# Centring the first tile ahead of its transposes, scaling it behind V, and loading V's weights in 256 KB chunks

## The chip, the cores and the metric

The kernel runs on one core of one Trainium2 chip. The metric is the device time of one execution in microseconds; the time before is the median of three runs. A core has a matrix engine (TensorE, PE in the profile; its weight loads are PEld), a vector engine (VectorE, DVE), a scalar engine (ScalarE, ACT), a general engine (GpSimd, POOL) and SyncE (SP), which here only issues DMAs. Each engine works through its own queue in order, and engines wait for each other through semaphores. Matrix products go to PSUM; from there VectorE or ScalarE copies them to SBUF.

## The reference

Two kinds of layer are applied twice in turn to x, which has 2048 tokens of 1024 features in bf16. Both have a layer norm without gain ahead of them and a residual addition behind them. Shapes are shortened here.

```
def _layernorm(x, eps=1e-5):
    return (x - mean(x)) / sqrt(var(x) + eps)

def _A_ref(x, wqkv, wo):          # 32 heads of 32, window of 8 keys, 2 tokens apart
    q, k, v = split_heads(x @ wqkv)
    logits = einsum("bhsd,bhswd->bhsw", q, gather(k)) * scale     # masked below token 0
    o = einsum("bhsw,bhswd->bhsd", softmax(logits), gather(v))
    return merge_heads(o) @ wo

def _B_ref(x, W_gate, W_up, W_down):
    gate = x @ W_gate
    h = gate * (gate > 0) * (x @ W_up)
    return h @ W_down

x = x + _A_ref(_layernorm(x), A_wqkv, A_wo)
x = x + _B_ref(_layernorm(x), B_W_gate, B_W_up, B_W_down)
x = x + _A_ref(_layernorm(x), A_wqkv, A_wo)
x = x + _B_ref(_layernorm(x), B_W_gate, B_W_up, B_W_down)
```

Only the first layer norm, of the first 512 tokens, and the V product behind it are touched by the change.

## The kernel before

The tokens are cut into tiles of 128 (`x_tiles`) and into blocks of four tiles; four blocks and two layer pairs make eight passes. In each pass come the norm, Q, K and V, the windowed attention on VectorE, the output projection, and the gated feed-forward. Weights come as slabs through a ring of five buffers (`load_slab`). The order of the work is written out by hand: every step is an event with a due time in us, the events are sorted, and each engine's instructions are chained in that order (`dv` for VectorE, `sp_dma` for SyncE's DMA queue, `pe_group` for TensorE, `on` in the first norm for ScalarE, GpSimd and VectorE).

The change lies in the start of block 0, where nothing can yet be overlapped. `load_x(0, ...)` fetches the first tiles of x; tile 0 comes in two halves, one on SyncE's queue and one on ScalarE's. The V weights come as two slabs `("v0", 0)` and `("v0", 1)`, each with four of the eight 128-row chunks of the contraction (`kc`), each in two DMAs of 512 KB.

`ln_first` normalises the four tiles of block 0. `scratch` issues matmuls on a constant while TensorE has nothing else. For tiles 0, 1 and 3, `bn` and `aggr` get mean and variance on VectorE; for tile 2, ScalarE gets the sum of squares and the mean (`act_square`, `act_mean`). `power` turns a variance into the reciprocal standard deviation (`rstd`) with two small GpSimd instructions. `apply` subtracts the mean and multiplies by `rstd` on VectorE, `turn` transposes the tile by eight TensorE transposes into PSUM, and `copy` brings the result to SBUF (`xnT`). Behind its matrices stand the second tile's transposes (`second`) and those of tiles 2 and 3 (`later`).

`v_first` then orders V's products so that they can begin with tile 0 alone. `prod(kc, c, t0, t1)` multiplies one contraction chunk by one of eight groups of 128 V columns (`c`) for tiles t0 to t1. `head` does contraction chunks 0 to 3 for tile 0 and slips in tile 1's transposes; `first_half(t)` does the same chunks for tiles 1, 2 and 3; `second_half(i, t0)` does chunks 4 to 7 for two tiles at once (256 columns) and ScalarE copies the finished accumulators out. The sums of tiles 0 and 1 share four PSUM buffers (`pairs`), those of tiles 2 and 3 four others; six buffers of that kind exist. After V come Q and K of block 0 (`qk_steps`), which read all four tiles of `xnT`, starting with Q's first column group.

In the chain of events the order of V's steps is: `head`, `first_half(1)`, `second_half(0..3, 0)` with tile 2's transposes ahead of i = 2, `first_half(2)` with tile 3's transposes in its middle, `first_half(3)`, `second_half(0..3, 2)`.

Of the kernel before, what the change touches and what calls it, by code (L numbers as in the profile page):

```python
# [8 lines left out]
F32 = mybir.dt.float32  # L9
ALU = mybir.AluOpType  # L10
ACT = mybir.ActivationFunctionType
AX = mybir.AxisListType

P = 128
D = 1024
# [5 lines left out]
KC = D // P  # L21
# [4 lines left out]
SLAB = 512  # L26
# [10 lines left out]
def kernel(  # L37
# [117 lines left out]
    eps_col = const.tile([P, 1], F32, name="eps_col")  # L155
    nc.gpsimd.memset(eps_col[:], EPS)
    NTOK = HALO + S
    v_d = dram.tile([H * DH, NTOK], BF16, name="v_d")
    o_d = dram.tile([NT, H, DH, P], BF16, name="o_d")
    q_d = dram.tile([KC, P, S], BF16, name="q_d")  # L160
# [10 lines left out]
    def load_x(b, tiles=range(TPB)):  # L171
        for t in (b * TPB + i for i in tiles):
            if t == 0:
                sp_dma(x_tiles[t][:, 0:SLAB], x_dram[t * P:(t + 1) * P, 0:SLAB])
                nc.scalar.dma_start(x_tiles[t][:, SLAB:D], x_dram[t * P:(t + 1) * P, SLAB:D])
            else:
                sp_dma(x_tiles[t][:], x_dram[t * P:(t + 1) * P, :])

# [41 lines left out]
    def load_slab(key, src):  # L220
        shp = list(src.shape)
        t = wring.tile([P, 8 * SLAB], BF16, tag="slab", name="w_" + "_".join(str(k) for k in key))
        tv = t[:, 0:shp[1] * shp[2]].rearrange("p (a b) -> p a b", b=shp[2])
        if key[0] == "v0":
            for i in range(2):
                rows = slice(i * (KC // 4), (i + 1) * (KC // 4))
                start = nc.scalar.dma_start if (key[1], i) == (0, 1) else sp_dma
                start(tv[:, rows, :], src[:, rows, :])
        else:
            sp_dma(tv, src)  # L230
        slab[key] = tv
# [69 lines left out]
        return mv, rstd  # L301

    load_slab(("v0", 0), qkv_half(2, 0))
    load_x(0, [2, 3])
    load_slab(("v0", 1), qkv_half(2, 1))
    load_slab(("qk01", "q", 0), qkv_half(0, 0))

# [3 lines left out]
    def scratch(count):  # L311
        sc = psum_l.tile([P, W, P], F32, tag="L", name="scratch")
        for _ in range(count):
            with pe_group():
                mm(sc[:, 0:WH, :], lhsT=ones[:, 0:P], rhs=ones[:], start=True, stop=True)

    def ln_first():
        hold = {"xnT": xnT_pool.tile([P, TPB, KC, P], BF16, tag="xnT", name="xnT_first")}
        xna = big_tile([P, TPB, D], "xn_first", True)
        last = {}  # L320

        def on(eng, f, *args, **kwargs):
            if eng == "v":
                dv(f, *args, **kwargs)
            elif eng in last:
                with tc.issue_after(last[eng]):
                    last[eng] = f(*args, **kwargs).ins
            else:
                last[eng] = f(*args, **kwargs).ins

        def small(name, bufs=4):
            return stat_pool.tile([P, 1], F32, tag="f" + name, name=name, bufs=bufs)

        mean, rstd, bst, sq = {}, {}, {}, {}

        def bn(t, half):
            if half == 0:
                bst[t] = stat_pool.tile([P, 2, 6], F32, tag="bst", name="bst")
            on("v", nc.vector.bn_stats, bst[t][:, half, :], x_tiles[t][:, half * SLAB:(half + 1) * SLAB])

        def aggr(t):
            mv = stat_pool.tile([P, 2], F32, tag="mv", name="mv", bufs=4)
            on("v", nc.vector.bn_aggr, mv[:], bst[t][:].rearrange("p a b -> p (a b)"))
            mean[t] = mv[:, 0:1]
            power(t, mv[:, 1:2], 1.0)

        def power(t, var, sign):
            rstd[t], vpe = small("rstd1"), small("vpe1")
            on("g", nc.gpsimd.tensor_scalar, vpe[:], var, sign, EPS, op0=ALU.mult, op1=ALU.add)
            on("g", nc.gpsimd.tensor_tensor, rstd[t][:], vpe[:], neg_half[:, 0:1], op=ALU.pow)  # L350

        def act_square(t):
            sq[t] = small("sq1")
            on("a", nc.scalar.activation, xna[:, t, :], x_tiles[t][:], ACT.Square, scale=float(D) ** -0.5,
               accum_out=sq[t][:])

        def act_mean(t):
            mn = small("mean1")
            on("a", nc.scalar.activation, xna[:, t, :], x_tiles[t][:], ACT.Identity, scale=1.0 / D, accum_out=mn[:])
            mean[t] = mn[:]  # L360

        def act_power(t):
            nvar = small("nvar1")
            on("v", nc.vector.scalar_tensor_tensor, nvar[:], mean[t], mean[t], sq[t][:], op0=ALU.mult, op1=ALU.subtract)
            power(t, nvar[:], -1.0)

        def apply(t, half=None):
            cols = slice(0, D) if half is None else slice(half * SLAB, (half + 1) * SLAB)
            on("v", nc.vector.tensor_scalar, xna[:, t, cols], x_tiles[t][:, cols], mean[t], rstd[t][:],
               op0=ALU.subtract, op1=ALU.mult)  # L370

        tps = {}

        def turn(t, halves=(0, 1)):
            if t in tps:
                pass
            elif t == 0:
                tps[t] = [psum.tile([P, KC // 2, P], BF16, tag="acc", name=f"tp{h}")[:] for h in range(2)]
            else:
                both = psum_l.tile([P, 2, KC, P], BF16, tag="L", name="tp_pair")  # L380
                tps[t] = [both[:, h, 0:KC // 2, :] for h in range(2)]
                if t == 1:
                    tps[t][1] = psum.tile([P, KC // 2, P], BF16, tag="acc", name="tp_second")[:]
            for c in (h * (KC // 2) + i for h in halves for i in range(KC // 2)):
                with pe_group():
                    tail_pe[0] = nc.tensor.transpose(tps[t][c // (KC // 2)][:, c % (KC // 2), :],  # L386
                                                     xna[:, t, c * P:(c + 1) * P], ident[:]).ins

        def copy(t, eng, h, i0=0, i1=KC // 2):
            f = nc.vector.tensor_copy if eng == "v" else nc.scalar.copy  # L390
            on(eng, f, hold["xnT"][:, t, h * (KC // 2) + i0:h * (KC // 2) + i1, :], tps[t][h][:, i0:i1, :])

        warm = small("warm")
        on("a", nc.scalar.activation, warm[:], ones[:, 0:1], ACT.Identity)
        scratch(13)
        bn(0, 0)
        bn(0, 1)
        aggr(0)
        bn(1, 0)
        apply(0, 0)  # L400
        apply(0, 1)
        turn(0)
        copy(0, "a", 0, 0, KC // 4)
        copy(0, "a", 0, KC // 4, KC // 2)
        act_square(2)
        act_mean(2)
        bn(1, 1)
        aggr(1)
        copy(0, "v", 1)
        apply(1, 0)  # L410
        apply(1, 1)

        def second(h):
            turn(1, (h,))
            copy(1, "v", h)
            if h == 0:
                return
            bn(3, 0)
            act_power(2)
            bn(3, 1)  # L420
            aggr(3)
            apply(2)
            apply(3)

        hold["second"], hold["last"] = second, last
        hold["later"] = {t: (lambda t=t: (turn(t), copy(t, "a", 0), copy(t, "v", 1))) for t in (2, 3)}
        return hold


# [2 lines left out]
    def v_steps(n, ln, key, early=False):  # L432
# [15 lines left out]

        return [f_(c) for c in range(KC)]

    def v_first(ln):
        st = att[0]
        pairs, opened = {}, set()
# [11 lines left out]

        def head():
            st["vT"] = big_tile([P, KC, BLK], "vT_0", True)
            for kc in range(KC // 2):
                for c in range(KC):
                    if (kc, c) == (KC // 2 - 1, KC // 2):  # L470
                        ln["second"](0)
                    prod(kc, c, 0, 1)
            ln["second"](1)

        def first_half(t):
            def f():
                for c in range(KC):
                    if t == 2 and c == KC // 2:
                        ln["later"][3]()
                    for kc in range(KC // 2):  # L480
                        prod(kc, c, t, t + 1)
            return f

        def second_half(i, t0):
            def f():
                if (i, t0) == (2, 0):
                    ln["later"][2]()
                for c in (2 * i, 2 * i + 1):
                    for kc in range(KC // 2, KC):
                        prod(kc, c, t0, t0 + 2)  # L490
                tail_act[0] = nc.scalar.copy(st["vT"][:, 2 * i:2 * i + 2, t0 * P:(t0 + 2) * P],
                                             pairs.pop((t0 // 2, i))[:]).ins
            return f

        tail = [(GRP * (2 + 4 * part + 0.5 * i), second_half(i, 2 * part)) for part in range(2) for i in range(KC // 2)]
# [598 lines left out]
```

## Time and profile before

| What | Value |
|---|---|
| median of three runs | 1618.01 us |
| lowest and highest run | 1617.66 and 1618.36 us |
| span of the profiled execution, first to last instruction | 1616.8 us |
| median less that span | 1.2 us |
| TensorE busy | 1610.6 us (100% of the span) |
| VectorE, ScalarE, GpSimd busy | 70%, 29%, 11% |
| TensorE busy from 0 to 24 us | 21.64 us |
| DMA share from 4 to 20 us, by stretches of 2 us | 1.02 to 1.06 |
| granted TensorE clock | 1.00 |

The profile shows one execution, whose own time is not given beside its span; the runs are taken without it, and 1.2 us lie between the span and their median. A row of the timeline begins with the start in us from the span's start and the duration; then come engine, line, operation, written tile and read tiles, shape, and the number of instructions merged. In brackets stands how long the engine was idle before, and what ended that. Line numbers are those of the code above; many operations share the line of a helper (L106 `dv`, L327 `on`, L132 `mm`). "Landing" of a DMA is counted from the start of its issue.

### The profile page before, as it was taken

The page shows a single profiled execution, that of the slowest core. Times are in us where ns is not written, and L with a number is a line of the kernel's source. Part 1 is how long each engine was busy: PE and PEld are TensorE (multiplying, and loading weights), DVE is VectorE, ACT ScalarE, POOL GpSimd, SP SyncE. Part 2 cuts the span into 40 slices and gives each one's busy share as a digit, 9 for nine tenths or more (in the row PEclk, how much of TensorE's full clock was granted, in tenths as well). Part 3 has the DMA queues.
Part 4 walks back from the last instruction along what each step waited for, and adds up shares of the span by engine and source line. Part 5 has one row for each costly group of instructions (what it writes and reads, how often), then busy time and mean ns, then how long its engine had stood idle before and what let it go on. Part 6 is the DMA issues. An engine that isn't in the chain of part 4 may idle for free.

```text
span 1616.8 us, 19042 instructions
## 1 busy us (share of the span) xinstructions
PE 1610.6 (100%) x7689; PEld 789.5 (49%) x7689; DVE 1138.9 (70%) x964; ACT 473.4 (29%) x964; POOL 180.5 (11%) x168
## 2 busy tenths in 40 slices
PE   9999999999999999999999999999999999999999
PEld 6646544444444445444454444544445444444445
DVE  6999979996989698929389293893939939311211
ACT  4753312132116313603136031361313311131110
POOL 3400100010003002300053000530005100000000
DMA  9767857596659666784747847489574874655452
GB/s 308 180 189 249 213 165 254 183 216 204 208 192 226 192 184 211 192 246 147 227 158 201 241 153 229 154 202 255 161 229 156 206 240 156 210 162 175 156 169 66
DMA packets 359065, 317.94 MB, mean 197 GB/s; under 512 B 105024, under 2 KB 332736, under 8 KB 358464
## 3 DMA queue, kind: packets, MB, share of 16 engines
q1 hardware_dynamic: 358272, 315.87, 67.2%
q8 instruction: 60, 0.98, 0.3%
q10 hardware_dynamic: 704, 0.85, 0.2%
q14 instruction: 29, 0.24, 0.1%
HBM read 266.29 MB, written 34.66 MB: 186 GB/s over the span
## 4 chain that ended last, share of the span: by engine, by line
PE 99%; DMA 1%; DVE 0%; ACT 0%; issue 0%; POOL 0%; DVEq 0%; SPq 0%; ACTq 0%
PE acc_u L132 24%; PE acc_g L132 24%; PE dacc L132 18%; PE acc_v L132 7%; PE acc_q L132 7%; PE acc_wo L132 7%; PE acc_k L132 6%; PE dacc_pair L132 6%; DMA w_o<-in_A_wo_dram 1%; DMA x<-in_A_x_dram 0%; PE tp_pair L386 0%; DVE x L848 0%; DVE bst L103 0%; DVE bst L106 0%; ACT kst L540 0%
## 5 line engine op out<-in xcount | busy, mean ns | idle before, releaser
L132 PE MATMUL acc_u<-xnT_b,w_u 128*128 128x512 bf16 x1792 | 423.3, 379 | 0.0
L132 PE MATMUL acc_g<-xnT_b,w_g 128*128 128x512 bf16 x1792 | 423.3, 379 | 0.0
L793 ACT ACTIVATE r<-acc_g 128x512 bf16<-128x512 f32 x224 | 133.6, 596 | 728.7 <-PE acc_g L132 699.4
L106 DVE TENSOR_TENSOR hT<-acc_u,r 128x512 bf16<-128x512 f32 x224 | 150.9, 686 | 241.7 <-PE acc_u L132 239.1
L132 PE MATMUL dacc<-w_d,hT 128*128 128x512 bf16 (+2 forms) x1428 | 302.0, 371 | 0.0
L132 PEld LDWEIGHTS <-hT 128*128 128x128 bf16 x1876 | 181.3, 98 | 206.0
L132 PEld LDWEIGHTS <-w_u 128*128 128x128 bf16 x1792 | 175.3, 98 | 211.4
L132 PEld LDWEIGHTS <-w_g 128*128 128x128 bf16 x1792 | 175.3, 98 | 211.4
L106 DVE TENSOR_TENSOR pv<-a,vhm 128x4096 bf16<-128x4096 bf16 x64 | 143.5, 2284 | 0.0
L848 DVE TENSOR_TENSOR x<-dacc,x 128x512 bf16<-128x512 f32 (+2 forms) x39 | 24.5, 659 | 154.3 <-PE dacc L132 154.3
L608 DVE TENSOR_TENSOR t<-q,k 128x2048 f32<-128x2048 bf16 x56 | 128.0, 2292 | 6.7 <-ACT k L543 4.6
L106 DVE TENSOR_TENSOR t<-q,k 128x2048 f32<-128x2048 bf16 x56 | 127.5, 2286 | 3.7 <-ACT k L543 2.6
L106 DVE TENSOR_TENSOR pv<-pv 128x1024 bf16<-128x1024 bf16 (+1 forms) x128 | 113.7, 950 | 0.0
L132 PE MATMUL acc_wo<-w_o,oT 128*128 128x512 bf16 x512 | 112.0, 379 | 0.6 <-DMA w_o<-in_A_wo_dram 0.6
L549 POOL COPY kh<-k 128x14 bf16<-128x14 bf16 x40 | 56.0, 1405 | 504.1 <-ACT k L543 504.1
L624 DVE TENSOR_TENSOR ac<-ac,t 128x2048 f32<-128x2048 f32 x48 | 109.7, 2284 | 0.3
L106 DVE TENSOR_TENSOR ac<-ac,t 128x2048 f32<-128x2048 f32 x48 | 109.7, 2284 | 0.0
L263 POOL TENSOR_TENSOR st_b<-st_b,neg_half 128x1 f32<-128x1 f32 x29 | 43.9, 1521 | 526.6 <-ACT st_b L262 526.6
L132 PE MATMUL dacc_pair<-w_d,hT 128*128 128x512 bf16 (+1 forms) x448 | 95.9, 366 | 0.0
L132 PEld LDWEIGHTS <-oT 128*128 128x128 bf16 x512 | 50.0, 98 | 61.2 <-DMA w_o<-in_A_wo_dram 1.1
L258 ACT ACTIVATE xn_b<-x 128x1024 bf16<-128x1024 bf16 x29 | 30.3, 1045 | 127.8 <-DVE x L106 65.7
L446 ACT CAST vT<-acc_v 128x512 bf16<-128x512 f32 x56 | 32.7, 586 | 57.3 <-PE acc_v L132 56.3
(136 smaller groups left out, 1228.0 us busy)
## 6 DMA issues: line engine op xcount, KB each, us to landing
w_g<-in_B_W_gate_dram SPq DMA_DIRECT2D x56, 1024.0 KB, 7.4
w_u<-in_B_W_up_dram SPq DMA_DIRECT2D x56, 1024.0 KB, 5.5
w_d<-in_B_W_down_dram SPq DMA_DIRECT2D x48, 1024.0 KB, 6.2
w_o<-in_A_wo_dram SPq DMA_DIRECT2D x16, 1024.0 KB, 8.1
vhm<-v_d SPq DMA_DIRECT2D x32, 284.0 KB, 6.7
v_d<-vT SPq DMA_DIRECT2D x8, 1024.0 KB, 10.0
oT<-o_d SPq DMA_DIRECT2D x32, 256.0 KB, 3.7
w_d<-in_B_W_down_dram SPq DMA_DIRECT2D x16, 512.0 KB, 3.9
```

Of the source, the lines that this page charges most:

```text
L106: tail_dve[0] = f(*args, **kwargs).ins
L132: tail_pe[0] = nc.tensor.matmul(*args, **kwargs).ins
L258: nc.scalar.activation(xn, xt[:], ACT.Square, accum_out=sq)
L263: nc.gpsimd.tensor_tensor(rstd, vpe, neg_half[:, 0:1], op=ALU.pow)
L446: tail_act[0] = nc.scalar.copy(st["vT"][:, c, :], acc[:]).ins
L549: nc.gpsimd.tensor_copy(khalo[n][:, c, :], k[:, BLK:BLK + HALO])
L608: nc.vector.tensor_tensor(t[:], i0, i1, op=ALU.mult)
L624: nc.vector.tensor_tensor(o, i0, i1, op=ALU.add)
L793: tail_act[0] = nc.scalar.activation(rs[j][:], acc[:], ACT.Relu).ins
L848: run = dv if n < NB - 2 else (lambda f, *args, **kwargs: f(*args, **kwargs))
```

## The change

Tile 0 is no longer normalised ahead of its transposes. VectorE and ScalarE each sum one half of it (scaled by 1/1024, so that the two parts add up to the mean), VectorE subtracts both parts, and the centred tile is transposed. Its variance is taken afterwards by ScalarE as the sum of squares of the centred tile; GpSimd's power follows. The `rstd` of its 128 tokens is stored to DRAM from ScalarE's queue (`r_d`) and read back so that every partition has all 128 values in a row (`rb`). VectorE multiplies V's sums of tile 0 by it as it takes them out of PSUM (`scaled`), and GpSimd multiplies tile 0 of `xnT` by it in place (`widen`) for Q and K. Scratch matmuls go from 13 to 9, and tile 2's statistics move from ScalarE to VectorE.

The V weights come by contraction chunk: six DMAs of 256 KB, then x tiles 2 and 3, then one DMA of 512 KB, all on SyncE's queue; x tile 1 moves to ScalarE's queue. `head` now does chunks 0 to 5 for tile 0, with tile 1's transposes around chunk 5; `first_half(1)` does chunks 0 to 5 for tile 1 chunk by chunk; `second_half` of tiles 0 and 1 does chunks 6 and 7. Tile 2's transposes move from i = 2 to i = 3. Tile 3's `apply` is placed between the first and second `scaled`. In `later` the two halves' copies change engines.

```
     def load_x(b, tiles=range(TPB)):
...
+            elif t == 1:
+                nc.scalar.dma_start(x_tiles[t][:], x_dram[t * P:(t + 1) * P, :])
...
         if key[0] == "v0":
-            for i in range(2):
-                rows = slice(i * (KC // 4), (i + 1) * (KC // 4))
-                start = nc.scalar.dma_start if (key[1], i) == (0, 1) else sp_dma
-                start(tv[:, rows, :], src[:, rows, :])
+            for i, (k0, k1) in enumerate(((0, 1), (1, 2), (2, 3), (3, 4)) if key[1] == 0 else ((0, 1), (1, 2), (2, 4))):
+                if (key[1], i) == (1, 2):
+                    load_x(0, [2, 3])
+                sp_dma(tv[:, k0:k1, :], src[:, k0:k1, :])
...
+        def centre():
+            parts = [small("part0"), small("part1")]
+            on("v", nc.vector.tensor_scalar, xna[:, 0, 0:SLAB], x_tiles[0][:, 0:SLAB], 1.0 / D, None, op0=ALU.mult,
+               op1=ALU.add, accum_out=parts[0][:])
+            on("a", nc.scalar.activation, xna[:, 0, SLAB:D], x_tiles[0][:, SLAB:D], ACT.Identity, scale=1.0 / D,
+               accum_out=parts[1][:])
+            for h in range(2):
+                cols = slice(h * SLAB, (h + 1) * SLAB)
+                on("v", nc.vector.tensor_scalar, xna[:, 0, cols], x_tiles[0][:, cols], parts[0][:], parts[1][:],
+                   op0=ALU.subtract, op1=ALU.subtract)
+
+        def spread_rstd():
+            sq = small("sq1")
+            on("a", nc.scalar.activation, xna[:, 1, :], xna[:, 0, :], ACT.Square, scale=float(D) ** -0.5,
+               accum_out=sq[:])
+            power(0, sq[:], 1.0)
+            hold["rb"] = stat_pool.tile([P, P], F32, tag="rb", name="rb", bufs=1)
+            on("a", nc.scalar.dma_start, bass.AP(tensor=r_d.tensor, offset=r_d.offset, ap=[[1, P], [1, 1]]), rstd[0][:])
+            on("a", nc.scalar.dma_start, hold["rb"][:], bass.AP(tensor=r_d.tensor, offset=r_d.offset, ap=[[0, P], [1, P]]))
+
+        def widen():
+            on("g", nc.gpsimd.tensor_tensor, hold["xnT"][:, 0, :, :], hold["xnT"][:, 0, :, :],
+               _ap(hold["rb"], 0, [[0, KC], [1, P]]), op=ALU.mult)
...
-        scratch(13)
-        bn(0, 0)
-        bn(0, 1)
-        aggr(0)
-        bn(1, 0)
-        apply(0, 0)
-        apply(0, 1)
+        scratch(9)
+        centre()
         turn(0)
         copy(0, "a", 0, 0, KC // 4)
         copy(0, "a", 0, KC // 4, KC // 2)
-        act_square(2)
-        act_mean(2)
+        copy(0, "a", 1)
+        spread_rstd()
+        bn(1, 0)
         bn(1, 1)
         aggr(1)
-        copy(0, "v", 1)
         apply(1, 0)
         apply(1, 1)
...
             copy(1, "v", h)
             if h == 0:
                 return
+            bn(2, 0)
+            bn(2, 1)
+            aggr(2)
             bn(3, 0)
-            act_power(2)
+            apply(2)
             bn(3, 1)
             aggr(3)
-            apply(2)
-            apply(3)
-
+
+        def later(t):
+            turn(t)
+            copy(t, "v", 0)
+            copy(t, "a", 1)
...
+    V_CUT = (6, 4)
...
-            for kc in range(KC // 2):
+            for kc in range(V_CUT[0]):
+                if kc == V_CUT[0] - 1:
+                    ln["second"](0)
                 for c in range(KC):
-                    if (kc, c) == (KC // 2 - 1, KC // 2):
-                        ln["second"](0)
                     prod(kc, c, 0, 1)
             ln["second"](1)
...
+        def scaled(i):
+            acc, rb = pairs.pop((0, i)), ln["rb"]
+            dv(nc.vector.tensor_tensor, st["vT"][:, 2 * i:2 * i + 2, 0:P], acc[:, :, 0:P], _ap(rb, 0, [[0, 2], [1, P]]),
+               op=ALU.mult)
...
-                if (i, t0) == (2, 0):
-                    ln["later"][2]()
+                if (i, t0) == (3, 0):
+                    ln["later"](2)
                 for c in (2 * i, 2 * i + 1):
-                    for kc in range(KC // 2, KC):
+                    for kc in range(V_CUT[t0 // 2], KC):
                         prod(kc, c, t0, t0 + 2)
...
+                if t0 == 0:
+                    ln["on"]("a", nc.scalar.copy, st["vT"][:, 2 * i:2 * i + 2, P:2 * P], pairs[0, i][:, :, P:2 * P])
+                    tail_act[0] = ln["last"]["a"]
+                    if i == 3:
+                        scaled(0)
+                        ln["apply3"]()
+                        for j in range(1, 4):
+                            scaled(j)
+                        ln["widen"]()
```

More of the change, by code (lines that the diff above doesn't have):

```diff
@@ L157 @@
     NTOK = HALO + S
+    r_d = dram.tile([1, P], F32, name="r_d")
     v_d = dram.tile([H * DH, NTOK], BF16, name="v_d")
@@ L303 @@
     load_slab(("v0", 0), qkv_half(2, 0))
-    load_x(0, [2, 3])
     load_slab(("v0", 1), qkv_half(2, 1))
@@ L332, in small @@
             return stat_pool.tile([P, 1], F32, tag="f" + name, name=name, bufs=bufs)
-        mean, rstd, bst, sq = {}, {}, {}, {}
+        mean, rstd, bst = {}, {}, {}
         def bn(t, half):
@@ L350, in power @@
             on("g", nc.gpsimd.tensor_tensor, rstd[t][:], vpe[:], neg_half[:, 0:1], op=ALU.pow)
[L352 to L365, printed above, removed]
+        def centre():
[19 more added lines that the diff above has]
+               _ap(hold["rb"], 0, [[0, KC], [1, P]]), op=ALU.mult)
         def apply(t, half=None):
@@ L417, in second @@
                 return
+            bn(2, 0)
+            bn(2, 1)
+            aggr(2)
             bn(3, 0)
-            act_power(2)
+            apply(2)
             bn(3, 1)
             aggr(3)
-            apply(2)
-            apply(3)
+        def later(t):
+            turn(t)
+            copy(t, "v", 0)
+            copy(t, "a", 1)
+        hold["widen"], hold["on"], hold["apply3"] = widen, on, lambda: apply(3)
         hold["second"], hold["last"] = second, last
-        hold["later"] = {t: (lambda t=t: (turn(t), copy(t, "a", 0), copy(t, "v", 1))) for t in (2, 3)}
+        hold["later"] = later
         return hold
@@ L476, in f @@
             def f():
+                if t == 1:
+                    for kc in range(V_CUT[0]):
+                        for c in range(KC):
+                            prod(kc, c, 1, 2)
+                    return
                 for c in range(KC):
                     if t == 2 and c == KC // 2:
-                        ln["later"][3]()
-                    for kc in range(KC // 2):
+                        ln["later"](3)
+                    for kc in range(V_CUT[1]):
                         prod(kc, c, t, t + 1)
             return f
+        def scaled(i):
+            acc, rb = pairs.pop((0, i)), ln["rb"]
+            dv(nc.vector.tensor_tensor, st["vT"][:, 2 * i:2 * i + 2, 0:P], acc[:, :, 0:P], _ap(rb, 0, [[0, 2], [1, P]]),
+               op=ALU.mult)
         def second_half(i, t0):
             def f():
-                if (i, t0) == (2, 0):
-                    ln["later"][2]()
+                if (i, t0) == (3, 0):
+                    ln["later"](2)
                 for c in (2 * i, 2 * i + 1):
-                    for kc in range(KC // 2, KC):
+                    for kc in range(V_CUT[t0 // 2], KC):
                         prod(kc, c, t0, t0 + 2)
-                tail_act[0] = nc.scalar.copy(st["vT"][:, 2 * i:2 * i + 2, t0 * P:(t0 + 2) * P],
-                                             pairs.pop((t0 // 2, i))[:]).ins
+                if t0 == 0:
[7 more added lines that the diff above has]
+                        ln["widen"]()
+                else:
+                    tail_act[0] = nc.scalar.copy(st["vT"][:, 2 * i:2 * i + 2, t0 * P:(t0 + 2) * P],
+                                                 pairs.pop((t0 // 2, i))[:]).ins
             return f
```

## The prediction

> **What bounds the kernel now.** I read the shares and the chain first.
>
> ```profile
> PE 1610.6 (100%) x7689; PEld 789.5 (49%) x7689; DVE 1138.9 (70%) x964; ACT 473.4 (29%) x964; POOL 180.5 (11%) x168
> ...
> PE 99%; DMA 1%; DVE 0%; ACT 0%; issue 0%; POOL 0%; DVEq 0%; SPq 0%; ACTq 0%
> ```
>
> TensorE is the bound from end to end, and the edit lies wholly ahead of its first Q matmul at 23.27 us. So the forecast is one number: when does that matmul start? From there on TensorE is full but for 0.6 us ahead of the output projection, and that weight is issued at 150.97 only after an eviction that TensorE itself set; a shift at 23.27 should reach the end one for one.
>
> The timeline of the first 24 us (start, duration, engine, line, operation) is therefore the view to work from.
>
> ```profile
> 1.52 4.43 PE L132 MATMUL scratch<-ones 128*128 128x512 bf16 x13 [1.52 <-DVE ones L309]
> ...
> 3.62 0.69 DVE L103 BATCH_NORM_STATS2 bst<-x 128x6 f32<-128x512 bf16 x1 [2.15 <-DMA x<-in_A_x_dram]
> ...
> 6.11 0.74 DVE L106 TENSOR_SCALAR xn_first<-x,mv,rstd 128x512 bf16<-128x512 bf16 x2 [0.41 <-POOL rstd L327]
> ...
> 6.58 0.72 PE L386 MATMUL tp<-ident,xn_first 128*128 128x128 bf16 x8 [0.63 <-DVE xn_first L106]
> ...
> 7.02 0.65 ACT L327 COPY xnT_first<-tp 128x256 bf16<-128x256 bf16 x2 [3.78 <-PE tp L386]
> ...
> 7.44 1.72 PE L132 MATMUL acc_v<-xnT_first,w_v 128*128 128x128 bf16 x28
> ...
> 7.75 1.06 ACT L327 ACTIVATE xn_first<-x 128x1024 bf16<-128x1024 bf16 x1
> 7.78 0.19 POOL L327 TENSOR_SCALAR vpe<-mv 128x1 f32<-128x1 f32 x1 [1.71 <-DVE mv L106]
> 8.06 0.55 POOL L327 TENSOR_TENSOR rstd<-vpe,neg_half 128x1 f32<-128x1 f32 x1
> 8.65 0.73 DVE L106 TENSOR_SCALAR xn_first<-x,mv,rstd 128x512 bf16<-128x512 bf16 x2 [0.66 <-POOL rstd L327]
> ...
> 9.12 0.40 PE L386 MATMUL tp_pair<-ident,xn_first 128*128 128x128 bf16 x4
> ...
> 10.03 3.69 PE L132 MATMUL acc_v<-xnT_first,w_v 128*128 128x128 bf16 x48
> ...
> 13.56 0.61 PE L386 MATMUL tp_pair<-ident,xn_first 128*128 128x128 bf16 x8
> ...
> 17.09 6.34 PE L132 MATMUL acc_v<-xnT_first,w_v 128*128 128x128 bf16 x80
> 23.27 5.34 PE L132 MATMUL acc_q<-xnT_first,w_qk_q 128*128 128x512 bf16 x24
> ```
>
> Tile 0 waits for statistics and the power (3.62 to 6.11), tile 1's transposes come at 9.12, and from 10.03 TensorE hardly stops. Two stretches give the prices: from 10.03 to 13.56 lie 32 products of 128 columns and 16 of 256, from 17.09 to 23.27 lie 48 and 32; so one of 128 costs 0.055 us and one of 256 costs 0.111.
>
> Then the DMA issues, one at a time (KB, us to landing), for x tile 0's second half and the V weights' first half:
>
> ```profile
> x<-in_A_x_dram ACTq DMA_DIRECT2D x1, 128.0 KB, 3.0
> ...
> w_v<-in_A_wqkv_dram SPq DMA_DIRECT2D x1, 512.0 KB, 5.3
> ```
>
> **The change, part by part.**
>
> *Cutting the products* costs nothing: half of 0.111 is 0.055.
>
> *Weights by 256 KB.* The queues land 1.5 MB by 7.0 us (1.72+5.3) and, with tiles 2 and 3, 2 MB by 8.3. With the new order that means contraction chunks 0 to 5 at about 5.0, 5.7, 6.4, 7.0, 7.65 and 8.3. Each chunk lasts TensorE 8 x 0.055 = 0.44. SyncE's extra issues (0.43 to 0.48 each) are quicker than the 0.65 a chunk takes. Tiles 2 and 3 now land some 1.5 us later than their 7.7 and 8.3, but are first read near 12: free.
>
> *Centring, the gain.* The second half of x lands at 3.80. ACT's half sum: the 1024-element pass takes 1.06, the 512-element evictions 0.585, so 0.6, and 0.1 that its accumulator read sticks out: 4.55. VectorE's half (between 0.41, the plain form, and 0.69, the statistics) ends earlier. First transpose 0.47 after the centring starts (6.11 to 6.58): 5.07. Scratch with 9 matmuls ends at about 5.15 (eight at 0.427, as the first ones go, then one at 0.216). I take 5.15 against 6.58: 1.43 us won, and V starts 0.86 later at 6.01. Its 40 products last 2.2: TensorE is ready for tile 1 at 8.2.
>
> *The new wait, the loss.* In program order tile 0's power now stands ahead of tile 1's on POOL, and it waits for ACT's square, which stands behind three copies. ACT: copies from 5.15+0.44 = 5.59 to 6.21, the third (0.59) to 6.84, square (1.06 + 0.1) to 8.05. POOL: tile 0's pair starts 0.09 later, at 8.14, and lasts 0.85, to 8.99; tile 1's pair, whose mean and variance are there since 7.1, runs 9.06 to 9.91. Apply at 9.95, transposes 0.47 later: 10.42, not 9.12. TensorE stands still from 8.2 to 10.42. By then it has done 40 products, not 28: 1.30 - 12 x 0.055 = 0.64 lost. The 0.26 that it idled around tile 1's transposes (9.12 to 10.03 holds 12 x 0.055 = 0.66 of work) is now filled by chunk 5's eight products: net loss 0.39 where tile 1's own products begin (11.30).
>
> *Behind it.* VectorE now does tile 2's statistics too (0.66 + 0.66 + 0.2) and four scalings (about 0.4 each, from the 0.686 of a 512-wide product out of PSUM), where ACT did the evictions. Followed in order: tile 1's copies to 11.92, tile 2's apply to 15.0 (its transposes are due at 15.23: no stall), statistics of tile 3 to 15.7, copy of tile 2 to 16.12 (stall 0.1), first scaling to 16.55, apply 3 at 16.7 (its power ends 16.65) to 17.25 (due 17.07: stall 0.23), three scalings to 18.4, copy of tile 3 to 18.85 (due 18.6: stall 0.3). Together 0.63; before had 0.16. Sum: 0.39 + 0.63 - 0.16 = 0.86 us. Q starts at 24.1.
>
> *The broadcast of rstd.* Not shown before: a 4-byte-per-partition store and its read back. ACT issues the store at 9.05 and is blocked in its queue until it has landed; behind it stands only V's eviction near 14.4. Nearest row: 3.0 from the ACT queue; far row: the 28 KB zero pad on SyncE's queue, 6.5. Two trips: 15.4 or 22.5. I take 3.0, as that queue holds nothing else. The first scaling is due at 16.15: hidden, with 0.75 to spare; past that the slip is one for one, since apply 3 and the transposes of tile 3 are queued behind it. DMA: Bandwidth & Descriptors (the Trainium skill, Anatomy of one DMA) speaks against the idea in that a write to HBM is acknowledged late and the semaphore waits for it; its 2.0 us a trip (given there for the other DMA path) would still land it by an estimated 13.5. No row here has a 4-byte store.
>
> *Widening on POOL.* From the row of the 128x128 select (0.28) and of a 14-wide memset (0.10) the slope is 1.6 ns: 1.7 us for 1024; up to 2.5 more if a long VectorE operation holds it, as one power took 2.53 at 38.35. It runs from 16.65 to between 18.4 and 20.9; Q at 24.1 is the cover. Block 1's powers and K's memsets queue behind it, with block 1 not used before 51 us.
>
> Sum against the profiled span: 1616.8 + 0.86 = 1617.7; the median lies 1.2 above the span, so 1618.9.
>
> **Rivals.** *The gain holds*: if tile 1's rstd is not held up (a square sooner, or VectorE's part smoother), its transposes come by 8.7, 0.4 earlier than before with 12 products more: 0.4 + 0.66 + 0.26 = 1.3 won, less 0.47 behind: 1617.2. The order of the code speaks against it. *rstd lands late*: by the far row at 22.5, 6.3 us beyond 16.15: 1618.9 + 6.3 = 1625.2. It decides over 0.2% (3.24 us) from a landing of 18.5, 4.7 a trip. The DMA share of 1.05 all through speaks for it, a queue of its own against. *The clock falls*: TensorE's stop grows from 0.63 to 2.2 us; the first eight scratch matmuls ran at 0.427, twice the later 0.216, so 3.4 us at that rate cost 1.7: 1620.6. In the rows nothing ran slow after 0.63. TensorE: Matmul & The Clock Gate (the Trainium skill, Part 1) has the clock fall after an idle window of about 3.4 us: by it this stop costs nothing.
>
> **How the numbers follow.** Forecast 0.65, its own span 1618.0 to 1619.7 (behind-work between 0 and 1.6); gain 0.20; late rstd 0.09; clock 0.06. Within 0.2% (3.24 us, about what a measurement of this kernel can tell from no change) lie the forecast, the gain and nearly all of the clock: 0.89. Slower 0.09. Faster 0.02: even with 1.43 won and every idle 0.1 to 0.3 filled it is under 3. The range reaches over the gain and most of the clock case: 1616.8 to 1620.5.
>
> **What would show it.** Right: first transpose near 5.15, an idle TensorE of about 2 us that ends with tile 1's apply at about 9.95, POOL's tile 0 power near 8.4, first Q matmul near 24.1. Wrong: tile 1's transposes before 9.2; a first scaling that waits for a DMA; matmuls of 0.427 pitch after 10 us; a Q matmul released by POOL.

## The result and the profile after

The changed kernel takes 1634.24 us (four runs, 1633.5 to 1635.24) against 1617.89 us: a ratio of 1.010 (1.0088 to 1.0112), 16.3 us slower. The span of the profiled execution goes from 1616.8 to 1631.8, by 15.0 us. Every execution whose time and span are both on record takes 1.66 to 1.79 us longer than its span: the span of 1616.8 belongs to a time of about 1618.5, at the upper end of the runs before, while the one of 1631.8 is that of the fastest changed run (1633.5), so the difference of the profiles is 1.3 us smaller than that of the medians. The prediction was 1618.9 with a range up to 1620.5; the time lies far outside it.

The page's shares and chain after:

```profile
PE 1610.1 (99%) x7651; PEld 791.9 (49%) x7701; DVE 1141.5 (70%) x968; ACT 472.2 (29%) x965; POOL 183.0 (11%) x169
...
PE 98%; DMA 1%; issue 0%; DVE 0%; ACT 0%; POOL 0%; DVEq 0%
```

TensorE's work is the same, but it is no longer full from end to end. The timeline (columns as before) shows where the hole lies:

```profile
5.34 1.06 PE L397 MATMUL tp<-ident,xn_first 128*128 128x128 bf16 x8
...
6.44 2.78 PE L132 MATMUL acc_v<-xnT_first,w_v 128*128 128x128 bf16 x40
...
9.16 0.34 ACTq L329 DMA_DIRECT2D r_d<-rstd  x1
...
10.55 0.40 PE L397 MATMUL tp_pair<-ident,xn_first 128*128 128x128 bf16 x4 [1.33 <-DVE xn_first L106]
...
20.30 0.38 ACTq L329 DMA_DIRECT2D rb<-r_d  x1
...
27.19 0.43 DVE L106 TENSOR_TENSOR vT<-acc_v,rb 128x256 bf16<-128x256 f32 x1 [10.67 <-DMA rb<-r_d]
27.23 2.13 POOL L329 TENSOR_TENSOR xnT_first<-xnT_first,rb 128x1024 bf16<-128x1024 bf16 x1 [10.47 <-DMA rb<-r_d]
27.53 2.17 DVE L106 TENSOR_SCALAR xn_first<-x,mv,rstd 128x1024 bf16<-128x1024 bf16 x1
...
29.75 1.03 PE L397 MATMUL tp_pair<-ident,xn_first 128*128 128x128 bf16 x8 [12.13 <-DVE xn_first L106]
30.58 7.91 PE L132 MATMUL acc_v<-xnT_first,w_v 128*128 128x128 bf16 x80
...
38.32 5.34 PE L132 MATMUL acc_q<-xnT_first,w_qk_q 128*128 128x512 bf16 x24
```

Tile 0 goes into its transposes at 5.34, tile 1 at 10.55, much as forecast. Then the store of `rstd` goes out at 9.16, its read back only at 20.30, and the first scaling comes at 27.19. Tile 3's apply stands behind that scaling, takes 2.17 us where it used to take 0.55, and TensorE has stood still for 12.13 us. Q starts at 38.32 instead of 23.27, 15.05 later: the whole difference of the spans.

The chain that ended last has the two trips as its two long pieces (start, length, what):

```profile
9.16 11.12 DMA r_d<-rstd
20.28 0.02 issue
20.30 6.79 DMA rb<-r_d
```

The stretches of two microseconds (length; busy us of PE, PEld, DVE, ACT, POOL; granted clock; DMA share; GB/s) show two more things:

```profile
12.00:14.00 2.00, 2.00 (x40) 2.00 (x37) 1.97 (x5) 0.00 (x0) 0.32 (x2) 1.00 1.07 393
14.00:16.00 2.00, 2.00 (x27) 1.85 (x25) 1.43 (x4) 0.00 (x0) 0.49 (x2) 1.00 1.44 95
16.00:18.00 2.00, 1.54 (x21) 1.17 (x18) 0.42 (x1) 0.00 (x0) 0.68 (x2) 1.00 1.00 44
...
20.00:22.00 2.00, 0.00 (x0) 0.00 (x0) 0.00 (x0) 1.28 (x5) 0.00 (x0) 0.55 0.73 185
22.00:24.00 2.00, 0.00 (x0) 0.00 (x0) 0.00 (x0) 0.41 (x2) 0.00 (x0) 0.50 0.81 306
```

From 14 us on the DMA engines are as busy as ever and move 95, then 44 GB/s instead of 393. And during the stop the granted clock (third from the end) falls to 0.50.

### The profile page after: what moved, and what is told of

The parts are those of the page before. It is cut to its first block, busy times and chain, and to the rows that moved or that the text cites. A ratio compares the mean times of both kernels' runs of the same rounds, so it can differ in the third digit from the quotient of the medians.

```text
span 1631.8 us, 19030 instructions
## 1 busy us (share of the span) xinstructions
PE 1610.1 (99%) x7651; PEld 791.9 (49%) x7701; DVE 1141.5 (70%) x968; ACT 472.2 (29%) x965; POOL 183.0 (11%) x169
## 4 chain that ended last, share of the span: by engine, by line
PE 98%; DMA 1%; issue 0%; DVE 0%; ACT 0%; POOL 0%; DVEq 0%
PE acc_u L132 24%; PE acc_g L132 24%; PE dacc L132 18%; PE acc_k L132 7%; PE acc_q L132 7%; PE acc_wo L132 7%; PE acc_v L132 6%; PE dacc_pair L132 6%; DMA r_d<-rstd 1%; DMA rb<-r_d 0%; PE scratch L132 0%; DVE xn_first L106 0%; ACT xnT_first L329 0%; PE tp_pair L397 0%; DVE x L883 0%
```

## The experiments

Theory: the trip of `rstd` through DRAM is the loss. Its rivals are other parts of the change (VectorE's added work, GpSimd's widening, the order of the loads); and inside the theory two mechanisms compete, a store that queues behind loads issued before it, and a store that is slow by itself.

**Without the trip.** `rstd` is spread to all partitions on TensorE, by ones times a diagonal matrix:

```
-            on("a", nc.scalar.dma_start, bass.AP(tensor=r_d.tensor, ...), rstd[0][:])
-            on("a", nc.scalar.dma_start, hold["rb"][:], bass.AP(tensor=r_d.tensor, ...))
+            on("v", nc.vector.tensor_scalar, hold["hi"][:], ident[:], rstd[0][:], None, op0=ALU.mult)
+            on("v", nc.vector.scalar_tensor_tensor, hold["lo"][:], ident[:], rstd[0][:], hold["hi"][:],
+               op0=ALU.mult, op1=ALU.subtract)
...
+            for i, part in enumerate(("hi", "lo")):
+                mm(ps[:], lhsT=ones[:, 0:P], rhs=hold[part][:], start=(i == 0), stop=(i == 1))
+            on("a", nc.scalar.copy, hold["rb"][:], ps[:])
```

> The changed kernel with the store of rstd and its read back taken out; tile 0's 128 values are spread to all partitions by two TensorE products of ones with a diagonal matrix (a bf16 part and the rest), copied to SBUF by ScalarE. Everything else is the changed kernel. If the trip through DRAM is all that went wrong, the first scaling starts near 16.5 us, TensorE does not stop after 11 us for more than 0.5 us at a time, the first Q matmul starts near 24.1 and the kernel takes 1618.9 us (1618.2 to 1619.7). If something else of the change costs time too (VectorE's added work, GpSimd's widening), it stays above 1621.

Measured: 1621.29 us (1.0020, 1.0011 to 1.0030). The trip, with what follows from it, is 13 of the 16 us, but not all: Q starts at 26.04, not 24.1. The rest is seen on VectorE and GpSimd in the timeline of this run:

```profile
16.60 0.41 DVE L106 TENSOR_TENSOR vT<-acc_v,rb 128x256 bf16<-128x256 f32 x1
...
16.89 2.13 POOL L328 TENSOR_TENSOR xnT_first<-xnT_first,rb 128x1024 bf16<-128x1024 bf16 x1
16.96 2.39 DVE L106 TENSOR_SCALAR xn_first<-x,mv,rstd 128x1024 bf16<-128x1024 bf16 x1
...
19.41 0.62 PE L408 MATMUL tp_pair<-ident,xn_first 128*128 128x128 bf16 x8 [1.61 <-DVE xn_first L106]
```

Tile 3's apply begins just behind GpSimd's widening and ends 0.3 us behind it, at 19.35; TensorE waits 1.61 us for it.

**Widening on VectorE.** The widening is issued on VectorE behind tile 3's copy, and nothing else changes against the kernel above:

```
-            on("g", nc.gpsimd.tensor_tensor, hold["xnT"][:, 0, :, :], hold["xnT"][:, 0, :, :],
+            on("v", nc.vector.tensor_tensor, hold["xnT"][:, 0, :, :], hold["xnT"][:, 0, :, :],
```

> The kernel that spreads rstd on TensorE, with the widening of tile 0 moved from GpSimd to VectorE, behind tile 3's copy. In that kernel tile 3's apply lasted 2.39 us while GpSimd widened, where tile 2's lasted 0.55. If the two hold each other up, the apply is back at 0.55, tile 3's transposes come 1.6 to 1.8 us sooner, the first Q matmul starts near 24.3 and the kernel takes 1619.6 us (1619.2 to 1620.0). If the apply is slow for another reason, it stays above 2 us and the time at 1621.3.

Measured: 1619.26 us (1.0008, 0.9999 to 1.0017). The two did hold each other up; the apply is short again and TensorE does not wait for it:

```profile
16.75 0.55 DVE L106 TENSOR_SCALAR xn_first<-x,mv,rstd 128x1024 bf16<-128x1024 bf16 x1
...
17.43 0.61 PE L408 MATMUL tp_pair<-ident,xn_first 128*128 128x128 bf16 x8
```

Q starts at 24.05. What is left of the change, with the spreading on TensorE in it, costs 0.78 us to there.

**A quiet queue.** Both DMAs of `rstd` go on SyncE's queue, and Q's and K's weights are issued only behind them:

```
-            on("a", nc.scalar.dma_start, ...)      # both
+            sp_dma(...)                            # both
...
-    load_slab(("qk01", "q", 0), qkv_half(0, 0))
...
     ln_a[0] = ln_first()
+    load_slab(("qk01", "q", 0), qkv_half(0, 0))
```

> The changed kernel with the same two DMAs of rstd issued from SyncE's queue, ahead of the Q and K weights, which are issued only behind them: when the store goes out near 9.2, only V's last chunk and tiles 2 and 3 are still on their way (to about 12). Backlog theory (the store waits behind 2 MB of weights that were issued before it, and the read behind the next ones): store landed by 14.5, read landed by 18, no slump of the DMA rate, kernel 1619 to 1622 us. Small-store theory (128 writes of 4 bytes are slow by themselves and hold up what follows): store 8 us or more from issue to landing, kernel 1627 us or more.

Measured: 1628.08 us (1.0063, 1.0048 to 1.0078). The issue of the store with its time to landing, and two of the stretches (columns as above):

```profile
r_d<-rstd SPq DMA_DIRECT2D x1, 0.5 KB, 7.6
```

```profile
12.00:14.00 2.00, 2.00 (x39) 2.00 (x37) 1.97 (x5) 0.00 (x0) 0.33 (x2) 1.00 0.00 0
14.00:16.00 2.00, 2.00 (x28) 1.85 (x25) 1.41 (x4) 1.11 (x3) 0.48 (x2) 1.00 0.03 8
```

The store goes out at 9.14 and lands 7.6 us later, the read at 16.74 and lands 5.8 us later, although the engines move at most 8 GB/s in every stretch from 12 to 20 us. The backlog alone explains neither. Why the read takes 5.8 us with so little else moving, where the 128 KB of x took 3.0, no run separates.

**Stores that nobody waits for.** Four probes add one store from ScalarE's queue, at 7.3 to 7.8 us, to the kernel before; only its shape differs:

```
+        on("a", nc.scalar.dma_start, bass.AP(tensor=r_d.tensor, offset=r_d.offset, ap=[[1, P], [1, 1]]), eps_col[:])
...
# 512 bytes a partition:   on("a", nc.scalar.dma_start, r_d[:], ones[:, 0:2 * P])
# 4 bytes, 512 apart:      ap=[[P, P], [1, 1]]
# 4 bytes, 64 apart:       ap=[[16, P], [1, 1]]
```

> The kernel before with one more DMA that nobody waits for: 128 partitions store 4 bytes each into 512 adjacent bytes of DRAM, from ScalarE's queue behind the copies of tile 0 (near 7.7 us), while Q's weights are queued. Small-store theory: the DMA rate falls under 100 GB/s for some 4 us a few us later and Q's first weights land later than the 9.4 us from issue of before. Backlog theory: it lands 8 to 11 us after its issue, with the rate unbroken near 390 GB/s and Q's weights landing as before. Time of the kernel within 1.5 us of before by both.

> As the kernel with the 4-byte store that nobody waits for, but each partition stores 512 bytes (64 KB in all). Small-store theory: no fall of the DMA rate, Q's weights land within 1 us of before. Backlog theory: issue to landing as with 4 bytes, 8 to 11 us. If any store to DRAM breaks the stream of loads, the rate falls here too.

> The kernel before with the 4-byte store that nobody waits for, but the 128 values go 512 bytes apart in DRAM instead of into 512 adjacent bytes. If it is the smallness of a write that stalls the stream, the DMA rate falls under 100 GB/s as with the adjacent store and the kernel takes 1621 us or more. If it is that 128 partial writes meet in the same few lines of memory, the rate stays above 300 GB/s, the store lands within 6 us, and the kernel takes 1617.5 to 1618.5 us.

> The kernel before with the 4-byte store that nobody waits for, with its values 64 bytes apart in DRAM, between the adjacent case (4 apart, rate broken, 1623.0 us) and the one 512 apart (rate unbroken, 1617.9 us). If the partial writes have to share 64 bytes or less to stall, the rate stays near 390 GB/s and the time at 1617.9. If they have to lie further apart, the rate falls as with the adjacent ones, in part or in full, and the time lies above 1619.

| Store | time | ratio to before | issue to landing |
|---|---|---|---|
| 4 bytes, adjacent | 1623.02 us | 1.0030 (1.0014 to 1.0045) | 13.2 us |
| 4 bytes, 64 apart | 1618.17 us | 1.0001 (0.9991 to 1.0011) | 5.2 us |
| 4 bytes, 512 apart | 1617.86 us | 1.0000 (0.9989 to 1.0010) | 5.1 us |
| 512 bytes, adjacent | 1617.98 us | 1.0000 (0.9990 to 1.0011) | 5.1 us |

The stretches with the adjacent store, and then those with 64 bytes between the values (columns as above):

```profile
12.00:14.00 2.00, 2.00 (x25) 1.84 (x23) 1.43 (x4) 0.56 (x1) 1.42 (x4) 1.00 1.69 204
14.00:16.00 2.00, 2.00 (x25) 1.83 (x23) 0.60 (x2) 1.46 (x4) 0.00 (x0) 1.00 0.58 11
16.00:18.00 2.00, 2.00 (x36) 1.96 (x34) 0.00 (x0) 0.96 (x3) 0.00 (x0) 1.00 1.96 49
18.00:20.00 2.00, 2.00 (x40) 2.00 (x38) 0.42 (x1) 0.43 (x1) 0.00 (x0) 1.00 1.01 39
```

```profile
14.00:16.00 2.00, 2.00 (x24) 1.84 (x23) 0.75 (x2) 1.47 (x4) 0.00 (x0) 1.00 1.05 388
16.00:18.00 2.00, 2.00 (x34) 1.94 (x33) 0.00 (x0) 0.96 (x3) 0.00 (x0) 1.00 1.05 386
```

Half a kilobyte that nobody reads breaks the stream of weights for 6 us and more and costs the kernel 5 us. The expectation of an unchanged time was wrong in that: Q's two halves landed 18.2 us (median) and K's first half 20.5 us after their issue, where it had been 10.8 and 13.5, and TensorE waited 2.5 us for K's. In this execution, the slowest of the four (1625.31), TensorE also stood for 1.67 us from 22.46, for a reason that the profile does not show. It is not the smallness of a write: the same 128 writes, 64 bytes apart, cost nothing. DMA: Bandwidth & Descriptors (the Trainium skill, Specifications) puts a read-modify-write on transfers under 512 bytes; that alone has no price here, 5.1 and 5.2 us for 4 bytes against 5.1 for 512. What costs is partial writes packed 4 bytes apart; 64 bytes apart is enough to avoid it here. Where between the two it begins, whether it matters how many writes meet in a larger stretch of memory (128 in the same 512 bytes, against 8 with 64 bytes between them), and where they are held up, no run shows.

**The trip kept, the packing gone.** In the changed kernel each partition stores its value 16 times, 64 bytes, and reads back all 8 KB:

```
+            on("g", nc.gpsimd.tensor_copy, wide[:], _ap(rstd[0], 0, [[0, 16]]))
-            ... bass.AP(tensor=r_d.tensor, offset=r_d.offset, ap=[[1, P], [1, 1]]), rstd[0][:])
+            on("a", nc.scalar.dma_start, r_d[:], wide[:])
```

> The changed kernel with the trip through DRAM kept, but each partition stores its rstd 16 times, 64 bytes, so that no two partitions write into the same 64 bytes; each partition reads back all 8 KB (1 MB in all, where it was 64 KB) and every 16th value is used. If the packed 4-byte writes are what stops the DMA engines in the changed kernel, the store lands 5 to 6 us after its issue instead of 11.1, the rate holds at 380 GB/s or more behind it, the first scaling starts between 20 and 24 us instead of 27.2, and the kernel takes 1625 to 1630 us. That would also leave 4 us or more of loss that any trip of this kind brings. If the packing is only a part of it, the store still lands after 18 us and the kernel stays above 1631.

Measured: 1630.11 us (1.0075, 1.0058 to 1.0092), at the upper end of what was expected. The chain of this run:

```profile
9.41 5.23 DMA r_d<-wide
...
14.65 8.24 DMA rb<-r_d
```

The store lands in 5.23, the rate stays at 386 GB/s or more from 12 to 22, and the first scaling comes at 22.99. Two trips under load are thus far too long even without the packing. The read carries 16 times the bytes here; with the 6.79 us of the changed kernel's read it would land near 21.4, an estimate, and still be late.

**The clock.** 52 matmuls on the constant fill TensorE's stop, and VectorE takes tile 2's second copy:

```
                     if t == 2 and c == KC // 2:
+                        scratch(52)
                         ln["later"](3)
```

> The changed kernel with 52 matmuls on the constant (0.216 us each, 11.2 in all) put into TensorE's long stop ahead of tile 3's transposes, and tile 2's second copy given to VectorE so that they can start near 17.6. The wait for rstd is left as it is, so what changes is the granted clock behind the stop. If the fallen clock is part of the loss, it stays 1.00, V's last 80 products take 6.2 us instead of 7.7, and the kernel gains 1.5 to 2.2 us on the changed one (1632 to 1632.8). If the clock made no difference, the time stays at 1634.

Measured: 1633.93 us (1.0098, 1.0078 to 1.0118), no gain that can be told. In this execution the store took 12.7 us, the scaling came at 29.14, and the filler ended at 28.84, 2.86 ahead of tile 3's transposes. That was enough for the clock to fall, as the stretches show (the granted clock is third from the end):

```profile
28.00:30.00 2.00, 0.84 (x4) 0.20 (x2) 0.86 (x2) 0.00 (x0) 0.82 (x1) 1.00 1.05 405
30.00:32.00 2.00, 0.30 (x4) 0.31 (x5) 2.00 (x3) 0.00 (x0) 1.36 (x2) 0.77 0.17 65
32.00:34.00 2.00, 2.00 (x21) 2.00 (x20) 1.86 (x5) 0.58 (x1) 0.00 (x0) 0.50 0.03 8
```

So the run did not hold the clock. Its price is read elsewhere: from tile 3's transposes to the first Q matmul lies the same work in all these kernels, 8.57 us in the changed one (29.75 to 38.32) and 6.62 with the clock at 1.00 (17.43 to 24.05, widening on VectorE): 1.95 us. The filled run lies between, as it should if the clock is the cause: its clock was back at about 34.5, after 2.8 us at half speed instead of some 4.1, and the same work took 7.95 us (31.70 to 39.65).

**The loads alone.** The kernel before with the new order and sizes of the V weights and of x's tiles 1 to 3:

```
+            elif t == 1:
+                nc.scalar.dma_start(x_tiles[t][:], x_dram[t * P:(t + 1) * P, :])
...
+            for i, (k0, k1) in enumerate(((0, 1), (1, 2), (2, 3), (3, 4)) if key[1] == 0 else ((0, 1), (1, 2), (2, 4))):
+                if (key[1], i) == (1, 2):
+                    load_x(0, [2, 3])
+                sp_dma(tv[:, k0:k1, :], src[:, k0:k1, :])
```

> The kernel before with the other half of the change alone: V's weights in six DMAs of 256 KB and one of 512 KB on SyncE's queue, x tile 1 on ScalarE's queue, x tiles 2 and 3 ahead of the last chunk. The statistics stay as they were, so the first product is due at 7.4 when chunks 0 to 3 have landed. Expected by all theories: 1617.9 us, within 0.5 of before. Over 1619 the new order of the loads would be a cause of its own.

Measured: 1618.93 us (1.0006, 0.9997 to 1.0015), a little above the expected half microsecond. The interval holds no change, but all ten runs (1618.74 to 1619.55) lie above all 27 of the kernel before that were taken with them (1617.65 to 1618.49). A loss of about 0.9 us is thus likely, though not more than that is shown; Q starts at 23.66, 0.39 later than before.

**Can the idea win?** Without trip and GpSimd, the order of the powers is next. Tile 1's statistics and power are put ahead of tile 0's:

```
-        spread_rstd()
         bn(1, 0)
         bn(1, 1)
         aggr(1)
+        spread_rstd()
...
-            on("a", nc.scalar.activation, xna[:, 1, :], xna[:, 0, :], ACT.Square, ...)
+            on("a", nc.scalar.activation, xna[:, 3, :], xna[:, 0, :], ACT.Square, ...)
```

> The kernel with rstd spread on TensorE and the widening on VectorE, with tile 1's statistics and power put ahead of tile 0's (the square writes its unused output to tile 3's place, the splitting of rstd and the products that spread it move behind tile 1's transposes). If GpSimd's order is what holds tile 1 up, its apply starts near 7.8 instead of 10.1, TensorE's stop ahead of tile 1's transposes goes, and the first Q matmul starts 1.2 us sooner than with tile 0 first: 1618.2 us (1617.6 to 1618.8). What is left behind it is VectorE's queue. If GpSimd's order does not matter, 1619.6.

Measured: 1618.32 us (1.0001, 0.9992 to 1.0011). Tile 1's apply starts at 7.58 instead of 10.08. TensorE's long stop there goes, and Q starts at 23.16. Tile 1's transposes come at 9.14, 1.6 behind the apply's start instead of 0.47: TensorE has not finished tile 0's 40 products before, and waits for V's weights on the way (0.25 us at 6.68). A part of the earlier start is thus lost again to the loads.

Then VectorE's queue, in two ways, each from this kernel on. First with tile 2's statistics on ScalarE, tile 3's apply straight behind tile 2's, and the third and fourth scaling behind tile 3's copy:

```
-            split_rstd()
-            bn(2, 0)
-            bn(2, 1)
-            aggr(2)
+            act_square(2)
+            act_mean(2)
             bn(3, 0)
-            apply(2)
+            split_rstd()
             bn(3, 1)
             aggr(3)
+            act_power(2)
+            apply(2)
+            apply(3)
```

> The kernel with tile 1's power first, with tile 2's statistics back on ScalarE (as in the kernel before), tile 3's apply straight behind tile 2's, and the third and fourth scaling moved behind tile 3's copy. If what is left of the loss is VectorE's queue ahead of tile 3's transposes, TensorE does not stop after 10 us for more than 0.2 us, the first Q matmul starts near 22.5 instead of 23.16 and the kernel takes 1617.5 us (1617.0 to 1618.0), a little under the kernel before. If TensorE's start is bound by the weights and not by VectorE, it stays at 1618.3.

Measured: 1619.12 us (1.0007, 0.9998 to 1.0016), the wrong way: tile 2's statistics on ScalarE and the order of the powers made its apply wait until 14.82, and TensorE 0.92 ahead of its transposes.

Second with the splitting of rstd on GpSimd:

```
             bn(3, 0)
-            apply(2)
             bn(3, 1)
             aggr(3)
+            apply(2)
+            apply(3)
...
-            on("v", nc.vector.tensor_scalar, hold["hi"][:], ident[:], rstd[0][:], None, op0=ALU.mult)
+            on("g", nc.gpsimd.tensor_scalar, hold["hi"][:], ident[:], rstd[0][:], None, op0=ALU.mult)
```

> The kernel with tile 1's power first and the widening on VectorE, with the splitting of rstd on GpSimd and both statistics of tile 3 ahead of tile 2's apply, tile 3's apply straight behind it. In the kernel it starts from, VectorE's queue made TensorE wait some 0.5 us ahead of tile 3's transposes. If that was the last loss, these transposes come near 15.9 instead of 16.53, the first Q matmul near 22.6 instead of 23.16 and the kernel takes 1617.8 us (1617.3 to 1618.2), level with the kernel before or a little under it. If the weights set the pace, it stays at 1618.3.

Measured: 1618.07 us (1.0001, 0.9992 to 1.0010). Tile 3's transposes come at 15.99 and Q starts at 22.61, both as expected, 0.66 earlier than in the profile of before. The time is level with the kernel before. No version that was run beats it.

## Why the prediction was wrong

The start of Q, from trace to trace, gives the account of the 15.05 us:

| Kernel | first Q matmul | step |
|---|---|---|
| before | 23.27 | |
| changed, without trip and without GpSimd's widening | 24.05 | 0.78 |
| the same with GpSimd's widening | 26.04 | 1.99 |
| changed, trip kept, packing gone | 34.68 | 8.64 |
| changed | 38.32 | 3.64 |

**The gain and the new wait: right in place and, with some luck, in size.** First transposes forecast at 5.15, found at 5.34; GpSimd's power of tile 0 at 8.4, found at 8.56; tile 1's apply at 9.95, found at 10.08; its transposes at 10.42, found at 10.55, after an idle stretch that the view of 8 to 10 us shows (TensorE busy 1.17 of 2). The sum of 0.86 us comes close to the 0.78 of the second line. This is not exact: the kernel of that line also spreads rstd on TensorE, which the prediction did not have, and by the medians it is 1.37 us slower than before, with an interval from no change to 2.8. Two terms were off and hidden: V's products start at 6.44 instead of 6.01, and the fifth chunk's products wait for their weights until 8.59, where 7.65 was forecast. So the 40 products end at 9.22 instead of 8.2 and the stop ahead of tile 1 is 1.33 us instead of 2.2; it ends on time because GpSimd's order ends it. That GpSimd's order holds tile 1 up is shown by the kernel that turns it round. The widening itself was bounded at 1.7 to 4.2 us and took 2.13.

**The term that failed: the broadcast of `rstd`.** It was put at 3.0 us a trip, from the row of x's second half on an empty machine, with 6.5 as the far end. The trips took 11.1 and 6.8. The near row was no row for these trips: it is a load of 128 KB that was issued with the DMA engines nearly idle (share 0.07 from 0 to 2 us), and the store goes out with the share at 1.03 from 8 to 10. Load is not the whole of it, as with the quiet queue the trips still took 7.6 and 5.8. The probes give a better row: 5.1 us for a small store at this place whose values lie 64 bytes or more apart, so 10.2 for two trips, if the read takes as long, and, by that step's own sum, a landing at 19.3 against the 16.15 that was due. The far end was too short as well, because packing the writes makes the store more than twice as long (11.1 against 5.2) and stops the loads; nothing in the trace of before could show that. (The 15.4 and 22.5 of that step also stand 0.35 and 0.45 above 9.05 and two trips, with no term named for it; nothing hangs on this.) Of the 8.64, 6.64 lie ahead of tile 3's transposes (19.41 to 26.05): the two trips, less what cover there was. The other 2.00 lie behind them, where the clock had fallen. The 3.64 are what the packing adds net of a read that was made longer (8.24 against 6.79).

**A wait priced on one side only.** GpSimd held by VectorE was allowed for, VectorE held by GpSimd was not. That cost the 1.99 us, as tile 3's apply (0.54 to 0.55 in the undisturbed rows) took 2.39. GPSIMD Engine Reference (the Trainium skill, Specifications) says that GpSimd shares its SBUF interface with VectorE and contends with VectorE's two-port modes and with instructions of two SBUF inputs; that page's line gives no price, and these rows do: 1.8 us for one apply. That the two operations hold each other up is shown by moving one of them; that the shared interface is where they do so, no run shows.

**The rivals.** The late rstd was the rival on the slow side, with 0.09: its mechanism and its place were right, its price of 6.3 us was less than half; its threshold (a landing past 18.5) was passed by so much, with 27.1, that nothing here tests it. The fallen clock was counted as a rival of its own, at 1.7 us; it came as a consequence of the late rstd and cost 1.95. TensorE: Matmul & The Clock Gate (the Trainium skill, Part 1) asks for about 3.4 us of idleness; here the clock fell about 2.6 us into the stop (0.55 in the stretch of 20 to 22 with a stop from 17.6), 2.2 us into the one of the filled kernel (28.84; 0.77 in the stretch of 30 to 32) and 3.3 us into the one with the quiet queue (17.6; 0.73 in the stretch of 20 to 22). With the adjacent store it fell near 34.8 although TensorE had only stopped for 0.90 and 1.62 us shortly before. So no single length of stop decides in these runs. The stop of 1.33 us ahead of tile 1 left the clock at 1.00.

**One for one.** The shift of Q did reach the end: 15.05 at Q, 15.0 in the span. For small shifts single profiles cannot tell, as the spans of the kernel before alone run from 1615.9 to 1617.4: with Q 0.66 earlier (22.61) the span fell by 0.7 and the median not at all, and with Q 0.70 later (23.97, the store 64 bytes apart) the span stayed at 1616.8. The 0.78 of the table is of this size too.

## What to carry to other kernels

Price a small DMA from a row of its own kind, at its place and under the load in which it will run, and count a store with a read behind it as two full trips; if a value per partition has to be spread over all partitions within 10 us, a product of ones with a diagonal matrix does it without a queue (9.15 to 10.37 us in the run without the trip). Do not scatter single values into adjacent bytes of DRAM while weights stream, even when nobody waits for them; 64 bytes between them were enough here. When work moves to an idle engine, ask what it does to its neighbour: a GpSimd operation in SBUF can be paid for by the VectorE operation beside it.

## What the hardware showed that was not expected

- 128 stores of 4 bytes into 512 adjacent bytes took the loads from 384 GB/s (10 to 12 us) down to 11 to 49 (14 to 20 us); the same stores 64 bytes apart left them at 386 and more.
- A store of 0.5 to 64 KB whose values were not packed took 5.1 to 5.2 us from issue to landing with the loads queued. The packed one took 11.1 to 13.2, and 7.6 where the loads ended 2 us behind its issue.
- A 1024-wide apply from SBUF to SBUF on VectorE took 2.16 to 2.49 us beside GpSimd's product of 2.13 to 2.63 us, against 0.55 alone.
- The clock fell 2.2 to 3.3 us after TensorE stopped, and once behind stops of only 0.90 and 1.62 us.
